# The end of a gated attention + MLP mixer kernel: last exponentials read from the PSUM banks, sums of the last unit by a selector product, and a general path written as a loop

## The chip, the cores and the metric

One Trainium2 chip, one NeuronCore of it. The metric is the device time of one execution in microseconds (us). A kernel is executed several times and the median is taken; one further execution is profiled, and its trace gives start and duration of each instruction.

The engines are PE (TensorE: matrix products into PSUM; a separate row, PEld, shows its weight loads), DVE (VectorE), ACT (ScalarE), POOL (GpSimd) and SP (SyncE, which here issues most DMAs). SBUF and PSUM have 128 partitions; PSUM is used as 8 banks of 128x512 fp32, called bank_1 to bank_8 below.

## The reference

```python
g = _sigmoid((x * gate_w).sum(-1, keepdims=True))
a = _A_ref(x, A_wq, A_wk, A_wv, A_wo)     # attention, 16 heads of 28, one shared k and v
b = _B_ref(x, B_w1, B_w2, B_w3, B_w4)     # layernorm, gelu, shifts by 1 and 2 tokens, MLP
return g * a + (1 - g) * b
...
# in _A_ref:
q = (x @ wq).reshape(B, S, H, Dh).transpose(0, 2, 1, 3)
scores = jnp.einsum("bhqd,bkd->bhqk", q, k) * (Dh ** -0.5)
p = _softmax(scores, axis=-1)
o = jnp.einsum("bhqk,bkd->bhqd", p, v)
```

x is 1 x 2048 x 448 fp32; the result has the same shape.

## The kernel before

The first 400 us or so compute the queries, the keys and values, and all of the branch b, which ends in the tile `x1`. The rest is attention. It runs over 16 **units**; unit u is one block of 512 queries (b = u // 4) for one group of four heads (g = u % 4). The four heads j = 0..3 lie on partitions 32j to 32j+31. A unit has 16 key tiles (kt) of 128 keys, taken two at a time: 8 **stretches** v per unit, 128 stretches in all, written out by the loop over k at L906.

In one stretch, for each kt, `scores` (L851) makes four banks of 128 keys x 512 queries, one for each head, with three products each (a split into high and low parts). `exps` then takes the exponentials: heads 0, 1 and 2 are read from the bank by ACT (L875, 128x512 each); head 3 (`DRAIN`) is copied by DVE from the bank into a tile `pd` (L872), and `late_exps` has ACT do the exponentials of both key tiles of head 3 in one instruction of 128x1024 (L880). `values` (L891) multiplies the exponentials by `vext`, the values with a first column of ones, so row 32j of the result holds the sum of the exponentials of head j. It makes 2 halves of 256 queries; each half is two key tiles times four heads, in fp32, into one bank, and DVE adds the bank to the tile `o` of the unit (L896). `values` of one stretch stands behind the scores of the next.

An fp32 product shows as two records of the PE in the trace (two passes). The four heads write different 32-column groups of the array, and their records overlap.

The finished `o` of unit u is normalised while unit u+1 runs (`sums_begin`, `recip`, `norm`) and multiplied by `wo` in half tiles of 128 tokens x 224 columns by `wo_half` (L813; DVE adds the result into `ot`, L821). Between the values of a stretch and the scores stand one or two of these half jobs; unit 14's eight half jobs stand in stretches 4 to 7 of unit 15.

**The end (L935 to L1016)**, for unit 15, which has no successor to hide behind:

- `values` of stretch 7, two banks (`pvs`), added to `o` in four pieces of 128 queries (L983);
- four PE transposes of `o` against `ident` (L988), so that tokens lie on partitions; reciprocals of the sums from the bank (L951), the product with them into `on4` (L955), four transposes back (L960), four ACT copies into `on` (L961);
- four `wo_job`s of 128 tokens x 448 columns (L813), with the final add on DVE for t = 0, 2, 3 (L971) and on ACT and POOL for t = 1 (L968, L969), and one output DMA each (L973): three issued by SP, one by ACT;
- `check` compares every sum with a limit (L783), `worst` is the least of the results (L1002), a PE transpose puts the 128 of them in a row (L1009), DVE makes the integer `redo` (L1012, L1013), and every engine loads it into a register (L1016) and branches on it (L1019);
- products of a bf16 tile of zeros into an unused bank stand between these steps (`keep_warm`, L980: 12 products).

If `redo` is not 0, all 16 units are computed again with exact row maxima (the **general path**). With these inputs it is not taken: every engine branches over it. It is written out for the 16 units, and stands in the program between the branch and the last few instructions. Counted in the built program, it holds 290 instructions for SP, 2,035 for ACT, 1,570 for DVE, 7,489 for PE and 104 for POOL. Behind it, in `if_false` and `end`, SP waits for its eight DMA semaphores, and the engines meet in a barrier (L1091 in the trace).

Order on each engine is that of the program text; the framework adds the semaphores. `tc.mark_branch_hint_location` at L985 puts one instruction on PE's queue (BRANCH_PREFETCH_HINT) that names the target of the later branch. The code between `with tc.block()` and its end stands in a block of its own, which every engine enters and leaves by an unconditional branch.

## Time and profile before

| | us |
|---|---|
| median of 3 runs | 925.17 |
| the three runs | 923.02, 925.17, 926.17 |
| the profiled execution, its own time | 922.61 |
| its span, first to last instruction | 920.8 |
| PE busy in the span | 909.2 |
| ACT busy | 634.7 |
| DVE busy | 542.2 |
| last exponentials of unit 15 end (L880) | at 905.32 |
| last computing instruction ends (DVE L971) | at 914.72 |

Times of single instructions are given as the start in us from the first instruction, so 905.32 is 15.5 us before the end of the span. The table shows that the median of the runs lies 2.56 us above the profiled execution, and that 1.81 us of the profiled time lie outside its span. Between the end of the last exponentials and the last computing instruction are 9.4 us; from there to the end of the span are 6.08 us, in which no engine computes.

### The profile page before, as it was taken

The numbers are of one execution on the slowest core, as the hardware profiler recorded it, in microseconds if no ns is written. First come the engines' busy times: TensorE is split into PE (matmuls) and PEld (weight loads), VectorE is DVE, ScalarE is ACT, GpSimd is POOL, SyncE is SP. The second block draws the span as 40 slices with busy tenths as digits, with TensorE's granted clock in tenths as the row PEclk, the third lists the DMA queues.
The fourth block names the chain that finished last, engine by engine and source line by source line (L and its number), as shares of the span: only waits on it lengthen the run. The fifth ranks groups of instructions, "written<-read, shape, count | busy, mean of one in ns | idle before, by whom it ended". The sixth has DMA issues, their size and how long they took to land. (4 is left out here: it accounts for less than half of the span.)

```text
span 920.8 us, 23987 instructions
## 1 busy us (share of the span) xinstructions
PE 909.2 (99%) x10039; PEld 643.9 (70%) x10039; DVE 542.2 (59%) x1081; ACT 634.7 (69%) x1134; POOL 105.9 (12%) x135
## 2 busy tenths in 40 slices
PE   9999999999999999999999999999999999999996
PEld 6788888888888888875555566555556555565653
DVE  4664264631435746446666676666666766766664
ACT  5542255322222131259999999999999999999993
POOL 2243200221000530031000000000000000000000
PEclk9999999999999999999999999999999999999999
DMA  9822543220221132110100101100011100110001
GB/s 307 296 65 47 160 147 114 40 66 21 41 70 50 37 97 62 26 60 18 26 25 3 25 15 56 24 26 26 11 37 46 26 6 22 36 45 3 14 14 44
DMA packets 41812, 51.85 MB, mean 56 GB/s; under 512 B 9312, under 2 KB 27552, under 8 KB 41696
## 3 DMA queue, kind: packets, MB, share of 16 engines
q1 hardware_dynamic: 38672, 44.77, 17.0%
q10 hardware_dynamic: 3024, 5.47, 1.7%
q8 instruction: 80, 1.31, 0.6%
q14 instruction: 36, 0.29, 0.1%
HBM read 37.04 MB, written 11.93 MB: 53 GB/s over the span
## 5 line engine op out<-in xcount | busy, mean ns | idle before, releaser
L875 ACT ACTIVATE p<-bank 128x512 f32<-128x512 f32 x768 | 391.0, 623 | 5.8 <-PE bank L851 5.8
L891 PE MATMUL bank<-p,vext 128*32 128x256 f32 x3072 | 243.9, 379 | 2.1 <-ACT p L875 2.1
L891 PE MATMUL bank<-pd,vext 128*32 128x256 f32 x1024 | 242.2, 379 | 0.3 <-ACT pd L880 0.3
L872 DVE COPY pd<-bank 128x512 f32<-128x512 f32 x256 | 176.7, 691 | 54.2 <-PE bank L851 52.5
L891 PEld LDWEIGHTS bank<-p,vext 128*32 128x32 f32 x3072 | 125.1, 110 | 85.8 <-ACT p L875 5.2
L664 ACT ACTIVATE gh<-g 128x512 fp32r<-128x512 f32 x55 | 32.9, 599 | 187.3 <-PE g L135 187.3
L896 DVE TENSOR_TENSOR o<-o,bank 128x256 f32<-128x256 f32 x222 | 93.5, 421 | 90.5 <-ACT p L875 51.0
L880 ACT ACTIVATE pd<-pd 128x1024 f32<-128x1024 f32 x128 | 142.5, 1113 | 0.0
L851 PE MATMUL bank<-qh,kH 30*128 30x512 f32 x1024 | 119.2, 444 | 0.0
L891 PEld LDWEIGHTS bank<-pd,vext 128*32 128x32 f32 x1024 | 111.6, 110 | 1.3 <-ACT pd L880 0.7
L666 DVE TENSOR_TENSOR gl<-gf,gh 128x512 fp32r<-128x512 f32 x55 | 37.9, 689 | 124.5 <-ACT gf L665 124.4
L851 PE MATMUL bank<-qh,kL 28*128 28x512 f32 x1024 | 105.1, 394 | 0.0
L851 PE MATMUL bank<-ql,kH 28*128 28x512 f32 x1024 | 104.4, 389 | 0.0
L851 PEld LDWEIGHTS bank<-qh,kH 30*128 30x128 f32 x1024 | 60.7, 182 | 58.4 <-ACT p L875 47.0
L675 PE MATMUL acc<-w4l,gh 128*128 128x448 f32 x220 | 80.4, 366 | 0.0
L674 PE MATMUL acc<-w4h,gh 128*128 128x448 f32 x220 | 80.3, 365 | 0.0
L676 PE MATMUL acc<-w4h,gl 128*128 128x448 f32 x220 | 80.1, 364 | 0.0
L813 PE MATMUL bank<-wof,on 128*32 128x224 f32 (+1 forms) x992 | 73.1, 370 | 0.3 <-ACT p L875 0.3
L132 PE MATMUL g<-al,w3h 128*128 128x512 f32 x168 | 65.8, 391 | 0.0
L131 PE MATMUL g<-ah,w3h 128*128 128x512 f32 x168 | 65.6, 391 | 0.0
L133 PE MATMUL g<-ah,w3l 128*128 128x512 f32 x168 | 65.5, 390 | 0.0
L851 PEld LDWEIGHTS bank<-ql,kH 28*128 28x128 f32 x1024 | 51.5, 185 | 9.2
(196 smaller groups left out, 1159.0 us busy)
## 6 DMA issues: line engine op xcount, KB each, us to landing
qd<-qf ACTq DMA_DIRECT2D x16, 256.0 KB
qm<-qd SPq DMA_DIRECT2D x16, 256.0 KB
qr<-qd SPq DMA_DIRECT2D x16, 256.0 KB
rb<-rd SPq DMA_DIRECT2D x15, 256.0 KB
x<-in_x_dram SPq DMA_DIRECT2D x4, 896.0 KB
xd<-xt SPq DMA_DIRECT2D x16, 224.0 KB
w34raw<-in_w_dram SPq DMA_DIRECT2D x7, 512.0 KB
out_dram<-ot SPq DMA_DIRECT2D x15, 224.0 KB
```

Source lines behind the costliest of these rows:

```text
L131: nc.tensor.matmul(ps, wh[:, c, :], ah[:, c, :], start=(c == 0), stop=False)
L132: nc.tensor.matmul(ps, wh[:, c, :], al[:, c, :], start=False, stop=False)
L674: nc.tensor.matmul(ps, gh[:, tok], w4h[i][:, k, :], start=(f == 0), stop=False)
L675: nc.tensor.matmul(ps, gh[:, tok], w4l[i][:, k, :], start=False, stop=False)
L676: nc.tensor.matmul(ps, gl[:, tok], w4h[i][:, k, :], start=False, stop=(f == stop))
L813: nc.tensor.matmul(ps[32 * j:32 * j + 32, cols], on_of[u][:, tok], wof[:, g, cols], start=True, stop=True, tile_position=(0, 32 * j))
L851: nc.tensor.matmul(bs[j], w, a, start=(i == 0), stop=(i == 2), tile_position=(32 * j, 0))
L872: nc.vector.tensor_copy(ps[j], bs[j])
L875: behind[kt % 2] = nc.scalar.activation(ps[j], bs[j], AF.Exp, scale=SCALE)
L880: ins = nc.scalar.activation(pd, pd, AF.Exp, scale=SCALE)
L891: nc.tensor.matmul(pv[32 * j:32 * j + 32, q], vext[:, kt, :], p_of[u, kt][j][:, q], start=(kt % 2 == 0), stop=(kt % 2 == 1), tile_position ...
L896: nc.vector.tensor_add(o_of[u][:, q], o_of[u][:, q], pv[:, q])
```

## The change

Everything up to the second last stretch is unchanged: the instructions of all five engines are the same up to there, but for five small POOL memsets that fill two constants at the start of the attention part. The loop stops one stretch earlier (L962 of the new file), and the last stretch and the end are written out anew.

- **Last stretch.** All four heads are read by ACT from the banks: four exponentials of 128x512 for key tile 14, then, for key tile 15, four of the first 256 queries and four of the last 256. The two DVE copies (L872) and the one exponential of 128x1024 (L880) are gone. The values of key tile 14 and of the halves of key tile 15 are separate steps. The half jobs 3 and 7 of unit 14 move behind them.
- **Sums and normalising.** `sel` is a 128x4 tile with ones at (32j, j). The product of a 128-token piece of `o` with `sel` gives the four sums with tokens on partitions. Two pieces make 8 columns, DVE takes their reciprocals and spreads them by a copy to 128x256 (`rx`), two PE products against `ident` bring them back into the layout of `o`, and DVE multiplies `o` by them straight into `on`. The transposes of `o`, the transposes back, the four ACT copies and the 12 `keep_warm` products are gone.
- **The flag.** The product of `worst` with a column of ones counts the tokens that pass; one DVE compare makes `redo`.
- **General path.** One unit (`redo_unit`) in a hardware loop `tc.For_i`, which keeps its running result in a DRAM tile. It holds 77 instructions for SP, 150 for ACT, 121 for DVE, 491 for PE and 29 for POOL between the branch and its target. It is still not taken with these inputs.

ACT, the last stretch. In the rows, p_ and pd_ are tiles of exponentials, bank_ the PSUM banks, and the words in brackets the engines whose semaphores are waited for. Before:

```order
L875 ACTIVATE p_3523<-bank_3504 128x512 [waits PE_49]
L875 ACTIVATE p_3524<-bank_3502 128x512 [waits PE_49]
L875 ACTIVATE p_3525<-bank_3505 128x512 [waits PE_49]
L875 ACTIVATE p_3526<-bank_3508 128x512 [waits DVE_49,PE_49]
L875 ACTIVATE p_3527<-bank_3506 128x512 [waits DVE_49,PE_49]
L875 ACTIVATE p_3528<-bank_3501 128x512 [waits DVE_49,PE_49]
L880 ACTIVATE pd_3536<-pd_3536 128x1024 [waits DVE_49,Activation_49]
```

With the change:

```order
L914 ACTIVATE p_3531<-bank_3504 128x512 [waits PE_49]
L914 ACTIVATE p_3532<-bank_3507 128x512 [waits PE_49]
L914 ACTIVATE p_3533<-bank_3502 128x512
L914 ACTIVATE p_3534<-bank_3505 128x512
L914 ACTIVATE p_3535<-bank_3508 128x256 [waits DVE_49,PE_49]
L914 ACTIVATE p_3536<-bank_3503 128x256 [waits DVE_49,PE_49]
L914 ACTIVATE p_3537<-bank_3506 128x256
L914 ACTIVATE p_3538<-bank_3501 128x256
L914 ACTIVATE p_3535<-bank_3508 128x256
L914 ACTIVATE p_3536<-bank_3503 128x256
L914 ACTIVATE p_3537<-bank_3506 128x256
L914 ACTIVATE p_3538<-bank_3501 128x256
```

Seven instructions became twelve over the same 4,096 columns; head 3's exponentials moved from the end of the queue to the second place of each group of four.

DVE, from the last add of unit 15 to the products with the reciprocals (o_ is the unit's unnormalised result, on_ the normalised one, rr_ the reciprocals, ot_ the output tiles). Before:

```order
L983 TENSOR_TENSOR o_10577<-o_10577,bank_3508 128x128 [waits DVE_49,PE_49,Activation_49]
L983 TENSOR_TENSOR o_10577<-o_10577,bank_3508 128x128
L983 TENSOR_TENSOR o_10577<-o_10577,bank_3503 128x128 [waits DVE_49,PE_49]
L983 TENSOR_TENSOR o_10577<-o_10577,bank_3503 128x128
L984 UNCONDITIONAL_BRANCH x2
L951 RECIPROCAL rr_10978<-bank_3506 128x8 [waits PE_49,Activation_49]
L955 TENSOR_TENSOR on_10979<-bank_3506,rr_10978 128x128 [waits DVE_49]
L955 TENSOR_TENSOR on_10979<-bank_3506,rr_10978 128x128
L951 RECIPROCAL rr_10978<-bank_3501 128x8 [waits PE_49,Activation_49]
L955 TENSOR_TENSOR on_10979<-bank_3501,rr_10978 128x128 [waits DVE_49]
L955 TENSOR_TENSOR on_10979<-bank_3501,rr_10978 128x128
```

With the change, where rx_ is the spread copy of the reciprocals:

```order
L940 TENSOR_TENSOR o_10585<-o_10585,bank_3502 128x256 [waits DVE_49,PE_49,Activation_49]
L827 SCALAR_TENSOR_TENSOR ot_9951<-bank_3504,gg,ot_9951 128x224 [waits PE_49]
L1005 RECIPROCAL rr_10909<-bank_3507 128x8 [waits PE_49]
L1006 COPY rx_10910<-rr_10909 128x256 [waits DVE_49]
L940 TENSOR_TENSOR o_10585<-o_10585,bank_3505 128x256 [waits PE_49,Activation_49]
L1016 TENSOR_TENSOR on_10908<-o_10585,bank_3502 128x128 [waits PE_49]
L1016 TENSOR_TENSOR on_10908<-o_10585,bank_3502 128x128
L1005 RECIPROCAL rr_10909<-bank_3504 128x8 [waits PE_49]
L1006 COPY rx_10910<-rr_10909 128x256 [waits DVE_49]
L1050 UNCONDITIONAL_BRANCH
L827 SCALAR_TENSOR_TENSOR ot_10187<-bank_3505,gg,ot_10187 128x224 [waits PE_49]
L1050 UNCONDITIONAL_BRANCH
```

The first half's reciprocals now stand ahead of the second half's add, two half jobs of unit 14 stand among them, and each reciprocal is followed by a copy.

PE, the same place with the change (the two products of exponentials with vext are the last values of unit 15):

```order
L819 MATMUL bank_3504<-wof,on_10723 32x224 [waits DVE_49]
L819 MATMUL bank_3504<-wof,on_10723 32x224 x3
L1003 MATMUL bank_3507<-sel,o_10585 128x4 [waits DVE_49]
L1003 MATMUL bank_3507<-sel,o_10585 128x4
L936 MATMUL bank_3505<-p_3535,vext 32x256 [waits Activation_49]
L936 MATMUL bank_3505<-p_3537,vext 32x256 [waits Activation_49]
L936 MATMUL bank_3505<-p_3538,vext 32x256 [waits Activation_49]
L936 MATMUL bank_3505<-p_3536,vext 32x256
L1012 MATMUL bank_3502<-ident,rx_10910 128x128 [waits DVE_49]
L1012 MATMUL bank_3502<-ident,rx_10910 128x128
L1003 MATMUL bank_3504<-sel,o_10585 128x4 [waits DVE_49]
L1003 MATMUL bank_3504<-sel,o_10585 128x4
```

The last values of the second half stand behind the selector products of the first, which wait for DVE.

The diff, cut:

```diff
+        sel = s3.tile([P, 4], F32, name="sel")
+        nc.gpsimd.memset(sel, 0.0)
+        for j in range(4):
+            nc.gpsimd.memset(sel[32 * j:32 * j + 1, j:j + 1], 1.0)
+        ones1 = s3.tile([P, 1], F32, name="ones1")
+        nc.gpsimd.memset(ones1, 1.0)
...
+        def redo_unit(i, acc, gd):
...
+        def last_exps(kt, bs, parts):
+            ps = p_of[NU - 1, kt] = {j: turn_of(p_free) for j in READ}
+            for q in parts:
+                for j in READ:
+                    nc.scalar.activation(ps[j][:, q], bs[j][:, q], AF.Exp, scale=SCALE)
...
+        def value(u, kt, q, pv):
+            for j in range(4):
+                nc.tensor.matmul(pv[32 * j:32 * j + 32, q], vext[:, kt, :], p_of[u, kt][j][:, q],
+                                 start=(kt % 2 == 0), stop=(kt % 2 == 1), tile_position=(0, 32 * j))
+
+        def add_value(u, q, pv):
+            nc.vector.tensor_add(o_of[u][:, q], o_of[u][:, q], pv[:, q])
+            banks.append(pv)
...
-        for k in range(NU * NV):
+        for k in range(NU * NV - 1):
...
         def tail_sums(i):
-            nc.vector.reciprocal(rr[:, i], sums_of(i))
-        def tail_on(t):
...
-        def tail_back(t):
...
+            ps = take()
+            for k in range(2):
+                nc.tensor.matmul(ps[:, 4 * k:4 * k + 4], o[:, toks[2 * i + k]], sel, start=True, stop=True)
+            sums = ps[:, 0:8].rearrange("p (k j) -> p k j", k=2)
+            nc.vector.reciprocal(rr[:, i], sums)
+            nc.vector.tensor_copy(rx[:, i], rr[:, i].unsqueeze(3).broadcast_to([P, 2, 4, 32]))
+            return sums, ps
+
+        def tail_spread(i):
+            ps = take()
+            for k in range(2):
+                nc.tensor.matmul(ps[:, toks[2 * i + k]], rx[:, i, k].rearrange("p j d -> p (j d)"), ident,
+                                 start=True, stop=True)
+            for k in range(2):
+                q = toks[2 * i + k]
+                nc.vector.tensor_mul(on_of[u][:, q], o[:, q], ps[:, q])
+            banks.append(ps)
...
+        bs = [scores(u, kt) for kt in (NT - 2, NT - 1)]
+        last_exps(NT - 2, bs[0], [slice(0, 512)])
+        banks.extend(bs[0][j] for j in READ)
+        last_exps(NT - 1, bs[1], HALVES)
+        values(u, v - 1)
+        pvs = [take(), take()]
+        for i, q in enumerate(HALVES):
+            value(u, NT - 2, q, pvs[i])
+        value(u, NT - 1, HALVES[0], pvs[0])
+        add_value(u, HALVES[0], pvs[0])
+        wo_half(u - 1, 3)
+        held = [tail_sums(0)]
+        value(u, NT - 1, HALVES[1], pvs[1])
+        add_value(u, HALVES[1], pvs[1])
+        banks.extend(bs[1][j] for j in READ)
+        tail_spread(0)
+        held.append(tail_sums(1))
         with tc.block():
             tc.mark_branch_hint_location("redo", "LikelyTaken", [mybir.EngineType.PE])
-            keep_warm(5)
...
+            wo_half(u - 1, 7)
+        tail_spread(1)
+        for i in range(2):
+            tail_check(i, *held[i])
         nc.vector.tensor_reduce(worst, good, axis=AX.XY, op=ALU.min)
...
+        wo_job(u, 0, end)
+        tw = bank("worst_t")[0:1, 0:1]
+        nc.tensor.matmul(tw, worst, ones1, start=True, stop=True)
+        nc.vector.tensor_scalar(redo, tw, P - 0.5, None, op0=ALU.is_lt)
+        for t in range(1, 4):
+            wo_job(u, t, end)
         again = nc.values_load(redo, min_val=0, max_val=1)
 
         with tc.If(again > 0, label="redo"):
-            for b in range(NB):
-                for g in range(NG):
...
+            acc = dram.tile([NB, 4, P, D], F32, name="acc")
+            gd = dram.tile([NB, P, 4], F32, name="gd")
+            nc.sync.dma_start(acc.rearrange("b t p d -> p (b t) d"), x1)
+            nc.sync.dma_start(gd.rearrange("b p t -> p b t"), gg.rearrange("p (b t) -> p b t", t=4))
+            with tc.For_i(0, NU, 1) as i:
+                redo_unit(i, acc, gd)
+            nc.sync.dma_start(out[0], acc.rearrange("b t p d -> (b t p) d"))
```

137 lines of the change are left out of this document (52 added, 85 removed).

## The prediction, made before the changed kernel ran

> **What bounds the kernel now.** I read the page first, then the timeline of the last 20 us, then the instructions on the line of the final branch, and last the DMA share behind the last computation. The page:
>
> ```profile
> span 920.8 us, 23987 instructions
> PE 909.2 (99%) x10039; PEld 643.9 (70%) x10039; DVE 542.2 (59%) x1081; ACT 634.7 (69%) x1134; POOL 105.9 (12%) x135
> ```
>
> PE is the bound over the whole. The change leaves 127 of 128 stretches alone, so only the end can answer. There the engines take turns, as the timeline shows (start us, duration, engine, line, count, idle before and its releaser):
>
> ```profile
> 901.33 3.05 ACT L875 ACTIVATE p<-bank 128x512 f32<-128x512 f32 x6 [0.29 <-PE bank L851]
> 902.00 0.96 PE L813 MATMUL bank<-wof,on 128*32 128x224 f32 x16
> 903.43 0.39 PE L891 MATMUL bank<-p,vext 128*32 128x256 f32 x3
> 903.64 0.39 PE L891 MATMUL bank<-p,vext 128*32 128x256 f32 x3
> 904.22 1.10 ACT L880 ACTIVATE pd<-pd 128x1024 f32<-128x1024 f32 x1
> 905.37 0.40 PE L891 MATMUL bank<-pd,vext 128*32 128x256 f32 x1 [0.25 <-ACT pd L880]
> 907.66 0.47 PEld L988 LDWEIGHTS bank<-ident,o 128*128 128x128 f32 x4
> 907.77 0.60 PE L988 MATMUL bank<-ident,o 128*128 128x128 f32 x4
> 908.25 0.21 DVE L951 RECIPROCAL rr<-bank 128x8 f32<-128x8 f32 x1 [0.46 <-PE bank L988]
> 908.50 0.49 DVE L955 TENSOR_TENSOR on<-bank,rr 128x128 f32<-128x128 f32 x2
> 908.84 0.33 PEld L960 LDWEIGHTS bank<-ident,on 128*128 128x128 f32 x2 [0.43 <-DVE on L955]
> 909.54 0.23 DVE L783 SCALAR_TENSOR_TENSOR good<-bank,good 128x8 f32<-128x8 f32 x2
> 909.80 0.19 DVE L1002 TENSOR_REDUCE worst<-good 128x1 f32<-128x32 f32 x1
> 909.96 0.96 PE L813 MATMUL bank<-wof,on 128*32 128x448 f32 x8
> 910.98 0.68 DVE L971 SCALAR_TENSOR_TENSOR ot<-bank,gg,ot 128x448 f32<-128x448 f32 x1 [1.00 <-PE bank L813]
> 912.19 1.71 PE L813 MATMUL bank<-wof,on 128*32 128x448 f32 x16
> 913.30 1.43 DVE L971 SCALAR_TENSOR_TENSOR ot<-bank,gg,ot 128x448 f32<-128x448 f32 x2 [0.48 <-PE bank L813]
> ```
>
> The last values wait for head 3's exponentials, which end at 904.22 + 1.10 = 905.32; the adds, transposes, reciprocals and four output jobs follow in a chain, and the last DVE instruction ends at 913.30 + 1.43 = 914.73. The span ends 6.08 us later. The instructions of the final branch show what fills that (duration min/median/max in ns, first and last start in us):
>
> ```profile
> L1019 SPq EVENT_SEMAPHORE  x8: 17/17/17, 918.9 to 919.4; - x8
> L1019 POOLq COMPARE_BRANCH  x1: 45/45/45, 913.4 to 913.4; - x1
> L1019 PEldq COMPARE_BRANCH  x1: 430/430/430, 913.5 to 913.5; - x1
> L1019 PEldq EVENT_SEMAPHORE  x1: 51/51/51, 914.0 to 914.0; - x1
> L1019 POOLq EVENT_SEMAPHORE  x1: 17/17/17, 914.0 to 914.0; - x1
> L1019 DVEq COMPARE_BRANCH  x1: 72/72/72, 914.7 to 914.7; - x1
> L1019 ACTq COMPARE_BRANCH  x1: 54/54/54, 915.1 to 915.1; - x1
> L1019 SPq COMPARE_BRANCH  x1: 45/45/45, 916.3 to 916.3; - x1
> L1019 DVEq EVENT_SEMAPHORE  x1: 21/21/21, 918.2 to 918.2; - x1
> L1019 ACTq EVENT_SEMAPHORE  x1: 17/17/17, 918.6 to 918.6; - x1
> ```
>
> From the branch to the first instruction behind it DVE needs 3.5 us, ACT 3.5, SP 2.6; POOL, which jumps over 104 instructions, 0.6, and PE, which was told the target, 0.5. DVE, ACT and SP jump over 1,570, 2,035 and 290. DVE and ACT wait there only for their own semaphore, long reached, so their 3.5 us is the price of the long jump. SP is last: 1.9 us of fixed work follows its 918.9.
>
> **The change part by part.** I build the new end from the same instant, 901.33.
>
> *Exponentials.* ACT gives a 128x512 every (904.22 - 901.33) / 6 = 0.48 us. Four for key tile 14 start up to 902.77, the next at 903.25. A 128x256 does not stand in the trace: half the 0.48 is 0.24; half of one whole 128x512 (0.62, below) is 0.31. I take 0.26: a 1024 costs 1.10 and a 512 0.62, so 256 columns more cost about 0.24, and the start-up is mostly hidden in the pitch. The first halves are then done at 903.25 + 4 x 0.26 + 0.1 = 904.4, the second at 905.45 (905.3 to 905.8). ACT's end is not earlier; what changes is that only two steps of values stand behind it.
>
> ```profile
> L875 ACT ACTIVATE p<-bank 128x512 f32<-128x512 f32 x768 | 391.0, 623 | 5.8 <-PE bank L851 5.8
> L896 DVE TENSOR_TENSOR o<-o,bank 128x256 f32<-128x256 f32 x222 | 93.5, 421 | 90.5 <-ACT p L875 51.0 <-PE bank L891 39.5
> L894 DVE COPY o<-bank 128x256 f32<-128x256 f32 x32 | 13.6, 424 | 14.2 <-ACT p L875 7.5 <-PE bank L891 6.7
> L821 DVE SCALAR_TENSOR_TENSOR ot<-bank,gg,ot 128x224 f32<-128x224 f32 x88 | 38.6, 442 | 0.0
> ```
>
> *PE up to the first half.* A step of values (four heads, one pass) takes 0.21 (903.43 to 903.64). From 902.00, where a half job gets its bank now, run 8 steps of stretch 6, 4 of key tile 14 and 2 of the first half: 14 x 0.215 = 3.0, last step issued at 904.8, done at 905.2. The exponentials of 904.4 are in time. DVE adds 0.42: 905.7. The two half jobs that stood at 902.00 (0.96 for both) fill PE's later waits; the two removed copies on DVE are off the path, since DVE waits for PE there.
>
> *Two rounds of sums and spread.* The selector product waits for that add: four loads of 0.117 (0.47 for 4, L988) and the drain, 0.6, so 905.8 to 906.4. Behind it on PE stand the second half's values (two steps, done 906.9), which cost nothing by ACT but wait here for DVE. DVE: reciprocal 0.21, copy 128x256 to rx. No such SBUF copy stands in the trace; the same size from a bank is 0.42, a floor is half of it, 0.21. I take 0.3: 907.0. Second add: 907.45. The spread is two fp32 products of 128 columns, four records like those of L988: 0.6, so 907.1 to 907.7; DVE's two products 0.49 (L955): 908.3. Second selector product 907.7 to 908.3, reciprocal and copy to 908.85; the half job of L1050 and its DVE part (0.44) to 909.3; second spread 908.95 to 909.6.
>
> *Output jobs.* PE takes 0.75 for each (0.96 with its drain). Job 0 follows the second spread: 909.55 to 910.3. DVE does the second pair of products (0.49, to 910.2), checks 0.23, worst 0.19: 910.65, then its add for job 0. PE's product with `worst` waits for that, and jobs 1 to 3 are queued behind it: start 910.85, last done at 910.85 + 3 x 0.75 + 0.2 = 913.3. The last DVE add, 0.68 with its start, ends at 914.1 to 914.2. Against 914.73 that is **0.55 earlier**. Bounds: 1.2 earlier if the copy and the short exponentials take the low ends and the handovers are as short as the 0.09 of L955 to L960; 0.6 later if copy (+0.12 twice) and exponentials (+0.2) take the high ends and the block's branches cost the 0.41 that PE lost there before:
>
> ```profile
> 907.21 0.44 PEld L980 LDWEIGHTS <-warm 128*128 128x128 bf16 x5 [0.41 <-issue]
> ```
>
> *The final branch.* DVE jumps over 121 instructions instead of 1,570, ACT 150, SP 77. POOL's jump over 104 took 0.6, so I price all three at 0.6. SP issues the last output, loads the flag and branches 1.6 us after DVE's end (914.73 to 916.3); with 0.6 it is at its DMA waits 2.2 us after, not 4.2. Then it may have to wait for the outputs to land:
>
> ```profile
> 915.00:916.50 1.50, 0.00 (x0) 0.00 (x0) 0.00 (x0) 0.00 (x0) 0.00 (x0) 1.00 0.99 358
> 916.50:917.00 0.50, 0.00 (x0) 0.00 (x0) 0.00 (x0) 0.00 (x0) 0.00 (x0) 1.00 0.54 189
> 917.50:918.00 0.50, 0.00 (x0) 0.00 (x0) 0.00 (x0) 0.00 (x0) 0.00 (x0) 1.00 0.05 18
> 918.00:918.50 0.50, 0.00 (x0) 0.00 (x0) 0.00 (x0) 0.00 (x0) 0.00 (x0) 1.00 0.00 0
> ```
>
> (The last two numbers are DMA share and GB/s; the 1.00 ahead of them is PE's granted clock.) The engines are full until about 916.7 and silent from 918.0, so the outputs land between 2.1 and 3.3 us after DVE's end. I take 2.6, which is nearer to the end of the full stretch than to the silence, since single late packets make up what follows 917.0: **1.6 earlier** than the 4.2 of now, bounds 0 and 2.0.
>
> The Trainium skill speaks here (Runtime: NRT & Kernel Launch, "Instruction fetch mechanics"): a taken branch whose target lies outside the current window of two pages forces a fetch of the target page, and a page is 16 KiB or 256 instructions. The rows agree with the rule for DVE and ACT. They differ on the page for these engines: queue q14 below moved 0.29 MB in 36 packets, 8 KB each, while q8 has 16 KB.
>
> ```profile
> q8 instruction: 80, 1.31, 0.6%
> q14 instruction: 36, 0.29, 0.1%
> ```
>
> *What is free.* The POOL memsets run at the start of attention, where POOL is 12% busy; `keep_warm` filled pauses of PE, and its loss costs nothing if the clock holds: after PE's last product at 913.9 the rows above still show 1.00 at 918.5, over 4 us later, and no pause of PE in my sum reaches 1 us.
>
> **Sum.** 0.55 + 1.6 = 2.15 us. The profiled execution would go from 922.61 to 920.5, its span from 920.8 to 918.65. The median of the runs is 2.56 above the profiled one, so 925.17 - 2.15 = **923.0**.
>
> **The rivals.**
>
> - *The branch gives nothing.* SP's 2.6 us would be the wait for the landing, or the fetch comes anyway. For it: SP's 290 instructions are far fewer than DVE's, and the row alone does not separate a jump from a DMA wait. Against it: DMA is silent from 918.0 and SP moves at 918.9. Only the 0.55 remains: 924.6. By the skill's 256 instructions a page, SP's target would lie in the next page already now, which speaks for this rival; by the 8 KB packets it would not.
> - *Both parts at their upper ends.* The chain in the end has less waiting than I count, and the outputs land soon after 2.2 us: 1.1 + 2.0 = 3.1, giving 922.1. For it: output 2 of 3 leaves earlier when the jobs run back to back.
> - *PE's clock falls* without the filler products. From the point where a pause is taken as idle, PE's work in the chain doubles: values 0.6, selector 0.6 and 0.6, spreads 1.2, half job 0.4, jobs 3.0, so up to 5 to 6 us more against 2.15 less: 928.5. Against it stands the 1.00 over 4 us of silence.
> - *It does nothing that shows:* the round trips between PE and DVE eat the end's 0.55 and the landing eats the branch: 925.2.
>
> **How the numbers follow.** Forecast 0.50, branch gives nothing 0.17, both upper ends 0.22, clock 0.06, nothing 0.05. What a measurement can tell from no change is about 0.3%, 2.8 us, so faster means under 922.4, slower over 927.9. Faster: all of the upper ends (0.22) and about three tenths of the forecast's cases, where a median of three strays by a us (0.15): 0.37. Slower: the clock and a trace of the rest: 0.07. Same: 0.56. The range: the bounds give 925.17 less 3.2 and plus 0.6, 922.0 to 925.8; the strength of the forecast's middle cuts the top to 925.4, and runs that spread over 3 us (923.02 to 926.17) widen the bottom to 921.0.
>
> **What would show it.** The instruction that follows the final branch starts within 0.7 us on DVE and ACT, and SP's eight waits begin 2.2 to 3 us behind the last DVE add. Twelve exponentials end near 905.5; the last add ends near 914.1; the granted clock stays 1.00; all before 901 is as it was. It is wrong if DVE and ACT still need over 2 us behind the branch, if SP's first wait alone lasts until 4 us after the add, or if the reciprocal-copy-spread rounds end later than 909.6.

## The result, and the profile after

| | before | after |
|---|---|---|
| median | 923.08 us (20 runs, 922.45 to 926.17) | 922.81 us (20 runs, 921.27 to 925.21) |
| ratio, 95% interval | | 0.9991 [0.9984, 0.9999] |
| the profiled execution | 922.61 us, span 920.8 | 921.29 us, span 919.5 |

By the ratio the change gains 0.83 us (0.0009 x 923.08), with 0.1 to 1.5 as its interval; the two medians differ by only 0.27. This is within the 0.3% below which the prediction counts a result as no change, the likeliest of its three cases (0.56). The median of before, 925.17 in the first three runs, is 923.08 over twenty.

The end of the changed kernel, DVE's part of its timeline (start, duration, engine, line, operation, tiles, idle time before it):

```profile
906.00 0.42 DVE L940 TENSOR_TENSOR o<-o,bank 128x256 f32<-128x256 f32 x1 [0.87 <-ACT p L914]
...
907.13 0.21 DVE L1005 RECIPROCAL rr<-bank 128x8 f32<-128x8 f32 x1 [0.34 <-PE bank L1003]
907.37 0.29 DVE L1006 COPY rx<-rr 128x256 f32<-128x256 f32 x1
907.80 0.42 DVE L940 TENSOR_TENSOR o<-o,bank 128x256 f32<-128x256 f32 x1
908.47 0.49 DVE L1016 TENSOR_TENSOR on<-o,bank 128x128 f32<-128x128 f32 x2 [0.25 <-PE bank L1012]
...
910.33 0.48 DVE L1016 TENSOR_TENSOR on<-o,bank 128x128 f32<-128x128 f32 x2 [0.42 <-PE bank L1012]
910.73 0.23 DVE L789 SCALAR_TENSOR_TENSOR good<-bank,good 128x8 f32<-128x8 f32 x2
911.00 0.19 DVE L1056 TENSOR_REDUCE worst<-good 128x1 f32<-128x32 f32 x1
...
913.05 1.44 DVE L1028 SCALAR_TENSOR_TENSOR ot<-bank,gg,ot 128x448 f32<-128x448 f32 x2 [1.05 <-PE bank L819]
```

ACT's part of the same timeline:

```profile
902.00 4.28 ACT L914 ACTIVATE p<-bank 128x512 f32<-128x512 f32 x12 [0.30 <-PE bank L896]
```

and PE's first selector products and second spread:

```profile
906.48 0.61 PE L1003 MATMUL bank<-sel,o 128*128 128x4 f32 x4 [0.22 <-DVE o L940]
...
909.51 0.71 PE L1012 MATMUL bank<-ident,rx 128*128 128x128 f32 x4
```

From the first exponential of the last stretch (902.00) to the end of the last DVE add (913.05 + 1.44 = 914.49) go 12.48 us by the unrounded times; before, 901.33 to 914.73, 13.39. This way is called the **body** below, and what follows the last add, up to the span's end, the **end**: 920.8 - 914.73 = 6.1 us before, 919.5 - 914.49 = 5.0 after. Body 0.91 earlier, end 1.05 earlier: 1.96, of which the span shows 1.3. The rest went ahead of the last stretch (below).

The instructions around the final branch, grouped by line (count, duration in ns, first and last start), in the changed kernel:

```profile
L1066 SPq EVENT_SEMAPHORE  x8: 17/17/17, 917.2 to 918.1; - x8
...
L1066 DVEq COMPARE_BRANCH  x1: 72/72/72, 914.4 to 914.4; - x1
L1066 DVEq EVENT_SEMAPHORE  x1: 21/21/21, 915.0 to 915.0; - x1
L1066 ACTq COMPARE_BRANCH  x1: 54/54/54, 915.3 to 915.3; - x1
L1066 SPq COMPARE_BRANCH  x1: 45/45/45, 916.7 to 916.7; - x1
L1066 ACTq EVENT_SEMAPHORE  x1: 17/17/17, 918.2 to 918.2; - x1
```

and SP's output DMAs, the durations being those of the issue (least, median, most):

```profile
L1030 SPq DMA_DIRECT2D out_dram<-ot x3: 338/344/1173, 912.0 to 914.5; - x3
```

DVE needs 0.6 us for its jump and SP 0.5, where they needed 3.5 and 2.6. ACT still needs 2.9. SP's last issue, 333 ns before, takes 1173. The last of SP's eight waits, the one for the last output, ends at 918.1, and 1.4 us of fixed work follow it, so this wait now sets the end. Windows of the DMA engines (the last three numbers are PE's clock, the DMA share and GB/s):

```profile
914.50:916.50 2.00, 0.00 (x0) 0.00 (x0) 0.00 (x0) 0.00 (x0) 0.00 (x0) 1.00 0.79 283
916.50:917.00 0.50, 0.00 (x0) 0.00 (x0) 0.00 (x0) 0.00 (x0) 0.00 (x0) 1.00 0.61 222
917.00:917.50 0.50, 0.00 (x0) 0.00 (x0) 0.00 (x0) 0.00 (x0) 0.00 (x0) 1.00 0.13 47
917.50:918.00 0.50, 0.00 (x0) 0.00 (x0) 0.00 (x0) 0.00 (x0) 0.00 (x0) 1.00 0.09 24
```

The engines carry much data until 917.0 and then a thin tail, single late parts of the last output. By the packet records the last of these ends at 917.67, and what is left after it is a packet of code; the semaphore for the last part comes at 918.12, 3.63 us behind the last add. This arrival of its last semaphore is meant below where an output **lands**.

**Ahead of the last stretch.** Two starts of the same instruction, the exponential of 128x1024 that stands once in each stretch, 110 stretches apart; before:

```profile
463.29 1.11 ACT L880 ACTIVATE pd<-pd 128x1024 f32<-128x1024 f32 x1
...
891.40 1.10 ACT L880 ACTIVATE pd<-pd 128x1024 f32<-128x1024 f32 x1
```

and after:

```profile
462.87 1.11 ACT L931 ACTIVATE pd<-pd 128x1024 f32<-128x1024 f32 x1
...
892.05 1.10 ACT L931 ACTIVATE pd<-pd 128x1024 f32<-128x1024 f32 x1
```

428.11 us before, 429.18 after. The changed kernel reached this part 0.42 earlier, lost 1.07 in it, and entered its last stretch 0.67 later. The 0.42 says nothing of the change: in two profiles of the kernel before, the first such exponential starts at 407.2 and at 408.8. Together: -0.42 + 1.07 + 0.02 - 0.91 - 1.05 = -1.3, the difference of the spans.

### The profile page after: what moved, and what is told of

Read it like the earlier page. It is cut to its first block, busy times and chain, and to the rows that moved or that the text cites. A ratio compares the mean times of both kernels' runs of the same rounds, so it can differ in the third digit from the quotient of the medians.

```text
span 919.5 us, 23981 instructions
## 1 busy us (share of the span) xinstructions
PE 909.0 (99%) x10036; PEld 643.5 (70%) x10036; DVE 541.9 (59%) x1078; ACT 635.0 (69%) x1135; POOL 104.5 (11%) x141
## 4 chain that ended last, share of the span: by engine, by line
PE 95%; ACT 3%; DVE 1%; DMA 0%; issue 0%; ACTq 0%; DVEq 0%
PE bank L936 23%; PE bank L896 21%; PE bank L819 7%; PE acc L675 5%; PE acc L674 5%; PE acc L676 5%; PE g L132 4%; PE g L131 4%; PE g L133 4%; ACT p L926 2%; PE hs L454 1%; PE hs L455 1%; PE g L135 1%; PE g L134 1%; PE h L131 1%; PE h L133 1%
```

## The experiments

All times of a run's body and end are from its own profile; each run's ratio is against runs of the kernel before on the same chip. The labels are the names in the table at the end of this section.

**body_only: the new end without the loop.** The general path is written out again, all else is as in the changed kernel.

```diff
         with tc.If(again > 0, label="redo"):
-            with tc.For_i(0, NU, 1) as i:
-                redo_unit(i, acc, gd)
+            for b in range(NB):
+                for g in range(NG):
+                    ...
```

> The changed end with the general path written out as before. Main theory: two separate gains. From the first exponential of the last stretch to the end of the last DVE add 12.5 us as with the change (13.4 before), and from there to the end of the span 6.1 us as before, with 2.5 to 3.5 us behind the final branch on SP, DVE and ACT; time about 0.9 us under before (ratio 0.999). Rival 1: the shorter program also shortens the end itself, then 13.4 returns. Rival 2, for the attention part: moving the tiles by 64 bytes makes each stretch slower, then the mean stretch is 3.90 us as with the change; if the drift is only from run to run, it can be anything from 3.88 to 3.91.

Measured: 923.96 us, ratio 1.000 [0.999, 1.0009]. Body 12.48, as with the change. SP's issues and the branch:

```profile
L1030 SPq DMA_DIRECT2D out_dram<-ot x3: 343/343/1301, 913.0 to 915.5; - x3
```

```profile
L1066 SPq EVENT_SEMAPHORE  x8: 17/17/17, 920.3 to 920.9; - x8
...
L1066 SPq COMPARE_BRANCH  x1: 45/45/45, 917.8 to 917.8; - x1
L1066 DVEq EVENT_SEMAPHORE  x1: 21/21/21, 919.0 to 919.0; - x1
```

The end is 6.77 us, not 6.1: SP's last issue takes 1.30 us instead of 0.33, SP reaches its branch later by that, and then pays the long jump, 2.5 us. So 0.5 to 0.7 of the new body's 0.9 is given back in the end (6.77 against 6.3 and 6.1 in the two profiles of the kernel before), to a slow issue that nothing in the diff names.

**loop_only: the old end with the loop.** The reverse edit: the end of the kernel before, the general path as `redo_unit` in a loop.

> The old end with the general path as a loop. Main theory: 13.4 us from the first exponential of the last stretch to the last DVE add as before, then 5.0 us or less to the end (6.1 before), with 0.5 to 0.7 us behind the branch on SP and DVE; ACT jumps over 137 instructions here and 150 with the change, so its 2.9 us may go or stay; ratio 0.999. Rival (the wait of SP is the landing of the output): 6.1 stays, ratio 1.000. Attention: the tiles stand at the old places, so 3.89 us per stretch if places matter.

Measured: 922.70 us, ratio 0.9984 [0.9973, 0.9994]. The body is 13.40 (903.37 to 916.76), the end 5.54, not the 5.0 or less of the main theory.

```profile
L1058 SPq EVENT_SEMAPHORE  x8: 17/17/17, 918.8 to 920.9; - x8
...
L1058 DVEq EVENT_SEMAPHORE  x1: 21/21/21, 917.3 to 917.3; - x1
L1058 SPq COMPARE_BRANCH  x1: 45/45/45, 918.3 to 918.3; - x1
L1058 ACTq EVENT_SEMAPHORE  x1: 17/17/17, 920.7 to 920.7; - x1
```

SP's jump takes 0.5 and its last issue 333 ns, so its eight waits begin 2.1 us behind the last add. They end at 4.2: SP now stands and waits for the last output. The loop does shorten the jumps of DVE and SP (ACT's, over 137 instructions, takes 3.6), and behind them lies the landing, not at 2.6 us but at 4.1 here.

The times of these two runs say something that the profiles of the end do not: the loop alone (0.9984) gains at least as much as the new end and the loop together (0.9991, and 0.9983 in a second measurement, below), and the new end alone gains nothing (1.000). The intervals overlap, so this is no more than a sign that the 0.9 us of the new body are lost again elsewhere in the kernel.

**hint_act: ACT is told the branch's target too.**

```diff
-            tc.mark_branch_hint_location("redo", "LikelyTaken", [mybir.EngineType.PE])
+            tc.mark_branch_hint_location("redo", "LikelyTaken", [mybir.EngineType.PE, mybir.EngineType.Activation])
```

> The changed kernel with the branch hint on ACT's queue too. Theory: ACT's 2.9 us behind the final branch are a fetch of instructions, and fall to 0.5 to 0.6. If ACT holds the end, the 5.0 us from the last DVE add to the end become 4.4 to 4.7, and the time is 0.3 to 0.6 us under the changed kernel; if SP's own chain (output, flag, eight DMA waits) holds it, 5.0 stays though ACT is early. Rival: ACT's 2.9 us wait for its output's transfer, then the hint changes nothing.

Measured: 922.13 us, ratio 0.9986 [0.9977, 0.9994]; body 12.48, end 5.06. ACT's jump still takes 2.7 us (915.6 to 918.3), and SP's last issue 1228 ns. A hint like PE's did nothing here for ACT; what it does for PE no run shows.

**old_places: the new small tiles behind the large ones in SBUF.** The allocations of `sel` and `ones1`, with their memsets, stand behind those of the `pd` tiles, so that the large tiles keep the addresses of the kernel before.

> The changed kernel with the two new constants allocated behind the tiles of exponentials, so that those stand at the addresses of before. If the move by 64 bytes made the stretches 3.90 instead of 3.89 us, they are 3.89 again and the time is about 1 us under the changed kernel (ratio 0.998 to before). If the drift was only from run to run, the time is that of the changed kernel (ratio 0.999).

Measured: 923.07 us, ratio 0.9987 [0.9974, 1.0001]; body 12.48, end 5.20. 49 stretches of attention (about 701 to 891 us in the kernel before) take 190.96 us, 190.53 in the kernel before, 191.06 in the changed one: the addresses of the tiles of exponentials are not what slows them.

**act_first: output job 0, not 1, over ACT and POOL.**

```diff
-            if t == 1:
+            if t == 0:
                 nc.scalar.activation(y, ps, AF.Copy, scale=gg[:, n:n + 1])
...
-            queue = nc.scalar if t == 1 else nc.sync
+            queue = nc.scalar if t == 0 else nc.sync
```

> Of the four output jobs the first, not the second, goes over ACT and POOL, so ACT issues its output about 1 us earlier and SP issues the other three. In the changed kernel ACT's issue starts 0.29 us before the last DVE add's end and SP's third issue, 0.32 us behind it, took 1.17 us instead of 0.34; in the kernel before, with 0.72 us between them, it took 0.33. Theory A (the third issue is slow because it comes right behind ACT's): SP's third issue takes 0.34 us, SP's eight waits begin 0.5 us or more earlier than 2.7 us behind the last DVE add, the last output lands up to 0.5 us earlier than 3.6 us behind that add, and the end (last DVE add to the span's end) goes from 5.03 to 4.5 to 4.9 us. Theory B (it is slow for another reason, such as a code fetch of SP): still about 1.2 us, end 5.0. Theory C (the issue is quick again but the landing is set by late packets): issue 0.34, end still 5.0. The way from the first exponential of the last stretch to the last DVE add stays 12.5 us in all.

Measured: 922.56 us, ratio 0.9987 [0.9979, 0.9996]; body 12.48, end 5.0.

```profile
L1030 SPq DMA_DIRECT2D out_dram<-ot x3: 338/434/1202, 914.4 to 916.3; - x3
```

One issue is still slow, now SP's second (1202 ns); the third takes 434. ACT's issue lay 0.7 us ahead of the slow one, as far as in the kernel before. Theory A falls; the numbers are those of theory B, whatever the reason.

**worst_late: the product with `worst` and the flag behind job 2.**

```diff
-        tw = bank("worst_t")[0:1, 0:1]
-        nc.tensor.matmul(tw, worst, ones1, start=True, stop=True)
-        nc.vector.tensor_scalar(redo, tw, P - 0.5, None, op0=ALU.is_lt)
-        for t in range(1, 4):
-            wo_job(u, t, end)
+        wo_job(u, 1, end)
+        wo_job(u, 2, end)
+        tw = bank("worst_t")[0:1, 0:1]
+        nc.tensor.matmul(tw, worst, ones1, start=True, stop=True)
+        nc.vector.tensor_scalar(redo, tw, P - 0.5, None, op0=ALU.is_lt)
+        wo_job(u, 3, end)
```

> The product with worst and the flag that DVE makes of it go behind the third output job instead of the first. Theory A: PE stood still from the end of job 0's issue (910.15 + 0.75 = 910.9) to 911.25 for DVE's worst; the jobs run back to back and the way from the first exponential of the last stretch to the last DVE add goes from 12.49 to 12.15 us. Theory B: job 0's products were only drained by 911.1 and the wait cost 0.15 at most: 12.35 to 12.5. The end stays 5.0 (third issue of SP about 1.2 us).

Measured: 922.55 us, ratio 0.9989 [0.9979, 1.0]. PE's three first jobs now run in one piece (its timeline):

```profile
910.71 2.46 PE L819 MATMUL bank<-wof,on 128*32 128x448 f32 x24
```

and the body is 12.17 us, 0.32 shorter, as theory A said. But the end is 5.9, not 5.0. All three issues of SP are quick (332 to 343 ns), and yet:

```profile
L1067 SPq EVENT_SEMAPHORE  x8: 17/17/17, 916.8 to 919.3; - x8
```

The last output lands at 919.3, 4.5 us behind the last add (914.73). What the DMA engines carried from 917.2 to 918.2 (queue and kind, packets, MB, share of 16 engines):

```profile
DMA packets 7, 0.03 MB, mean 32 GB/s; under 512 B 1, under 2 KB 5, under 8 KB 5
...
q8 instruction: 1, 0.02, 6.0%
q1 hardware_dynamic: 5, 0.01, 4.9%
q14 instruction: 1, 0.01, 2.6%
```

Five packets of output stand beside two of code. By the packet records, the q8 packet (PE's, 16 KB; PE's load of the flag came 1.8 us later here against the last add, and with it PE's branch) ran from 917.22 to 918.18 for 0.96 us, where a row of the output takes 0.074; the last row of the output started at 918.17, as that packet ended. This fits a last output that waited behind a packet of code; that both stood on the same DMA engine is not shown, since the records do not name the engine.

**pad_act: ACT's branch 42 instructions further on in its code.** Nothing of the computation depends on the added copies.

```diff
             nc.vector.tensor_sub(gl, gf, f32(gh))
+            if b == NB - 1:
+                for i in range(3):
+                    nc.scalar.copy(pad[:, 1 + f:2 + f], pad[:, 0:1])
             return gh, gl
```

> 42 tiny ACT copies are added in the last block of the third weight stage (three behind each gf), where ACT waits 3.85 us for PE each time, so that ACT's final branch lies 42 instructions further on in its code. The general path that it jumps over stays the same 150. Theory A (a jump is quick where the target lies in the present or the next piece of 128 instructions, the 8 KB of a q14 packet; ACT's 150 cross two borders from where it stood, DVE's 121 and SP's 77 only one): ACT moves on 0.6 us behind the branch instead of 2.9. The end stays at 5.0, because the landing of the last output bounds it, or gains up to 0.4 us where the fetch no longer shares the DMA engines with the outputs. Theory B (150 is too far wherever it starts, or ACT waits for something else): 2.9 us again. The copies themselves cost under 0.1 us on the path.

Measured: 922.68 us, ratio 0.999 [0.9981, 1.0]; body 12.48, end 4.96.

```profile
L1072 SPq EVENT_SEMAPHORE  x8: 17/17/17, 918.8 to 919.6; - x8
...
L1072 ACTq COMPARE_BRANCH  x1: 54/54/54, 916.8 to 916.8; - x1
L1072 ACTq EVENT_SEMAPHORE  x1: 17/17/17, 917.3 to 917.3; - x1
```

ACT jumps over the same 150 instructions in 0.5 us instead of 2.9. So not the distance alone decides, but where in its code the branch stands, as theory A has it. By the packet records no packet of code comes between ACT's branch and its next instruction here; in the changed kernel two of q14 do, though the records do not say for which engine. The end hardly moves, since ACT is not what SP waits for last.

The Trainium skill (Runtime: NRT & Kernel Launch, "Instruction fetch mechanics") says that a taken branch stalls if its target is outside the present window of two pages. This run agrees with that rule. The page size that it gives, 16 KiB or 256 instructions, would make a jump of 150 quick from any place, if the window is the present page and the next. With half of that, the 8 KB of a q14 packet, the changed kernel and this run both fit, if the borders lie so that the 150 instructions crossed two of them and cross one now. Where the borders lie no run shows, so the 8 KB are a guess that fits.

**early_load: the flag is loaded into the registers right behind its product**, ahead of jobs 1 to 3; only the branch stays at the end.

```diff
         nc.vector.tensor_scalar(redo, tw, P - 0.5, None, op0=ALU.is_lt)
+        again = nc.values_load(redo, min_val=0, max_val=1)
         for t in range(1, 4):
             wo_job(u, t, end)
-        again = nc.values_load(redo, min_val=0, max_val=1)
```

> The engines load the flag of the final branch into their registers right behind its product, ahead of output jobs 1 to 3, instead of behind them; only the branch itself stays at the end. In seven profiles SP's issue was slow (0.9 to 1.3 us) just where another engine's load of the flag began 0.05 us behind the start of that issue while outputs were under way (ACT's load at the third issue, DVE's at the second where the first job goes over ACT), and quick (0.33) where the load had begun before it. Theory A (the load that begins during the issue holds it up): SP's third issue 0.34 us, SP at its branch 0.5 us behind the last DVE add instead of 2.2, its eight waits from 1.0; the landing of the last output, 3.4 to 3.6 us behind the add so far, then shows alone: 2.5 to 3.5, the end 4.0 to 5.0 us instead of 5.03. Theory B (the issue waits for room in the queue or for something else): third issue still 0.9 to 1.3 us, SP's waits from 2.0 on. ACT's exponent-free job 1 starts 0.3 us later by its load, which is off the path. From the first exponential of the last stretch to the last DVE add 12.5 us.

Measured: 923.74 us, ratio 0.9992 [0.9981, 1.0003]. SP's issues are all quick (333 to 342 ns) and its waits begin 0.9 us behind the add; the last output lands at 3.3, the end is 4.7. But the body is 13.78. PE's timeline shows where that went:

```profile
912.70 0.19 PE L1059 MATMUL bank<-ones,worst 128*1 128x1 f32 x2
914.04 2.46 PE L819 MATMUL bank<-wof,on 128*32 128x448 f32 x24 [1.15 <-DVE redo L1060]
```

PE has to load the flag as well, and its jobs 1 to 3 stand behind that load: 1.15 us of waiting, which the expectation did not see.

**best_a: early_load, act_first and pad_act together.**

> The early load of the flag, the first output job over ACT and POOL instead of the second, and the 42 copies that put ACT's final branch further on, together. ACT then branches about 1 us before the last DVE add and its jump needs no code from outside its window, so the only instruction packets left beside the last output are those of PE and of the program's end. Theory A (late packets of the last output are those that queue behind instruction fetches on the same DMA engine): all 16 parts of the last output land by 2.5 to 2.9 us behind the last DVE add instead of 3.4 to 3.6, end 4.0 to 4.4 us, time about 0.8 us under the changed kernel's. Theory B (late packets come anyhow): landing 3.4 to 3.6, end 4.9 to 5.1. Body 12.5 us in both.

Measured: 923.95 us, ratio 1.0001 [0.9989, 1.0013]. Body 13.47 (the same wait of PE, 0.84 us), end 4.15.

```profile
L1072 SPq EVENT_SEMAPHORE  x8: 17/17/17, 918.7 to 920.6; - x8
```

The last add ends at 917.83, so the last output lands 2.75 us behind it. Here PE's code packet had ended 0.8 us ahead of the last add, ACT's jump was quick (0.5 us), and the windows show no tail:

```profile
917.85:919.85 2.00, 0.00 (x0) 0.00 (x0) 0.00 (x0) 0.00 (x0) 0.00 (x0) 1.00 0.72 260
919.85:920.35 0.50, 0.00 (x0) 0.00 (x0) 0.00 (x0) 0.00 (x0) 0.00 (x0) 1.00 0.05 18
920.35:920.85 0.50, 0.00 (x0) 0.00 (x0) 0.00 (x0) 0.00 (x0) 0.00 (x0) 1.00 0.00 0
```

The end is the one that theory A forecast; the body eats the gain. But the records give another reason than theory A's. The last output lands in 16 parts, each with its own semaphore record. In the changed kernel the middle one of them lands 2.69 us behind the last add and the last one 0.94 later; here it is 1.86, and the last one 0.89 later. So the late parts trail as they did before, and the whole output lands 0.83 earlier, just as much as SP's last issue ends earlier (0.36 us behind the add instead of 1.20). The quick issue alone is not enough, though: in early_load it ends at 0.36 too, and the middle part lands at 2.36. There ACT's output was issued 0.3 us ahead of the last add, here 2.4 us.

**best_b: the same, with `worst`, flag and load behind job 1.**

> As the kernel before in this list, with the product with worst, the flag and its load put behind the second output job instead of the first, so that PE does not stand still for DVE (0.32 us, as the run with that product behind the third job showed: 12.17 us instead of 12.49). PE's own branch, and with it its 16 KB instruction packet, come about 0.5 us later against the last DVE add than in the changed kernel (where the packet ran from 0.53 before the add to 0.45 behind it), and still ahead of the last output's packets. Theory A: body 12.17 us, end as that of the kernel before in this list (4.0 to 4.4). Theory B (SP's load of the flag now sits between its first and second issue and delays the outputs, or PE's packet meets the last output as it did when the product stood behind the third job): body 12.17, end 4.8 us or more.

Measured: 924.64 us, ratio 1.0005 [0.9993, 1.0016]. Landing 2.8, end 4.2 as in best_a, though SP's last issue took 689 ns; body 13.78, since PE waits 1.46 us for the flag, now ahead of jobs 2 and 3. The stall moved with the load. SP's issue, though slower than in best_a, ended 0.72 us behind the add, and the middle part landed at 2.23: again 1.5 us behind the end of the issue, as in the changed kernel and in best_a.

**after_again and before_again: both kernels once more, unaltered.**

> The changed kernel once more, unaltered, to see how far its own profile repeats. In its first profile the attention's stretches came every 3.899 us against 3.890 in the kernel before, 1.1 us over the whole. Theory A (this is a difference between executions): another pitch, anywhere between 3.887 and 3.90, and a time ratio of 0.9975 to 0.9985. Theory B (the change costs the attention 1.1 us): 3.899 again. In both: first exponential of the last stretch to last DVE add 12.49 us, end 5.0, SP's third issue 1.2 us.

> The kernel before once more, unaltered. The attention's stretches came every 3.890 us in its first profile and 3.888 in the one kernel with the old end, but every 3.893 to 3.900 in eight profiles of kernels with the new end. Theory A (a difference between executions): anywhere from 3.887 to 3.90. Theory B (the new end costs the attention 0.5 to 1.1 us): 3.888 to 3.891 again. First exponential of the last stretch to last DVE add 13.40 us, end 6.0 to 6.2.

Measured: the changed kernel 922.10 us, ratio 0.9983 [0.9973, 0.9993], body 12.48, end 4.9, SP's last issue 933 ns. The kernel before, in one profiled execution, 924.40 us, body 13.40, end 6.3, SP's last issue 713 ns. The 49 stretches took 190.88 and 190.51 us, 3.896 and 3.888 each: the kernel before repeats its pitch, and every kernel with the new end is slower, as theory B of before_again has it.

All profiles in one table (us; the last output's middle and last part and PE's packet of code against the end of the last DVE add; the parts are by the semaphore records, since SP does not wait for them everywhere):

| kernel | 49 stretches | body | end | SP's last issue | last output: middle part | last part (lands) | PE's packet |
|---|---|---|---|---|---|---|---|
| before | 190.53 | 13.39 | 6.1 | 0.33 | 2.4 | 3.6 | -0.1 to 1.1 |
| before_again | 190.51 | 13.40 | 6.3 | 0.71 | 2.4 | 4.0 | 0.5 to 1.5 |
| loop_only | 190.54 | 13.40 | 5.5 | 0.33 | 2.4 | 4.1 | 0.7 to 1.6 |
| after | 191.06 | 12.48 | 5.0 | 1.17 | 2.7 | 3.6 | -0.5 to 0.5 |
| after_again | 190.88 | 12.48 | 4.9 | 0.93 | 2.5 | 3.4 | -0.6 to 0.3 |
| body_only | 190.81 | 12.48 | 6.8 | 1.30 | 2.8 | 3.9 | -0.4 to 0.7 |
| hint_act | 190.80 | 12.48 | 5.1 | 1.23 | 2.7 | 3.7 | -0.5 to 0.5 |
| old_places | 190.96 | 12.48 | 5.2 | 1.28 | 2.8 | 3.8 | -0.4 to 0.6 |
| act_first | 190.85 | 12.48 | 5.0 | 0.43 (second 1.20) | 2.6 | 3.6 | -0.9 to 0.2 |
| worst_late | 191.09 | 12.17 | 5.9 | 0.33 | 2.4 | 4.5 | 2.5 to 3.5 |
| pad_act | 191.06 | 12.48 | 5.0 | 1.29 | 2.8 | 3.6 | -0.6 to 0.7 |
| early_load | 191.07 | 13.78 | 4.7 | 0.33 | 2.4 | 3.3 | -1.8 to -0.9 |
| best_a | 191.06 | 13.47 | 4.2 | 0.33 | 1.9 | 2.8 | -1.8 to -0.8 |
| best_b | 191.09 | 13.78 | 4.2 | 0.69 | 2.2 | 2.8 | -0.7 to 0.4 |

No kernel here is clearly faster than the changed one. One that has the quick landing of best_a without PE's wait was not tried.

## Why the prediction came out as it did

The forecast was 923.0 us and the median 922.81. That they agree is luck: the base was 2.1 us too high, the gain was forecast too large by more than 1 us, and the two misses offset each other.

**The base.** "The median of the runs is 2.56 above the profiled one" rested on three runs. Over twenty it is 0.47 above (923.08 against 922.61). With this base the forecast gain of 2.15 would have given 920.9, below the stated range. Against the profiled execution the forecast was 920.5 and the measurement 921.29, so 0.8 of the gain is missing there, and 1.3 by the ratio (2.15 - 0.83).

**The body: right in its mechanism, its size too small.** 0.55 was forecast, 0.91 came, and within 0.02 of it in all seven profiles with the change's order of products and jobs. The instruction prices held to about 0.1 us: selector product 0.61 (0.6 taken), copy 0.29 (0.3), spread 0.71 (0.6); the second spread was done 8.22 us behind the first exponential (910.22 - 902.00; forecast 909.6 - 901.33 = 8.27). What was sized wrong is the way from there on: the checks and `worst` were done at 9.19 (forecast 9.32), job 1 could start at 9.25 (forecast 9.52), and the last add ended 0.78 us behind PE's last product. For this step the prediction says 0.68, yet goes from 913.3 to 914.1 or 914.2, 0.1 to 0.2 more than its own figures give. The copy and the short exponentials took their middle values, not the bounds. PE's clock stayed at 1.00 without the filler products, as taken, through the end of all fourteen profiles; but the reason given for it, the 4 us of silence at 1.00, was weaker than it looked (last section).

**The final branch: the mechanism right on DVE and SP, wrong on ACT.** DVE's jump went from 3.5 to 0.6 us, SP's from 2.6 to 0.5. "I price all three at 0.6" failed for ACT, 2.9 us: in pad_act the same 150 instructions took 0.5 from another place, which fits a jump past the code that was already there. By the prediction's own test ("It is wrong if DVE and ACT still need over 2 us behind the branch") this step fell for ACT. It cost little, because SP's wait for ACT comes behind the landing: with ACT quick the end was 4.96.

**The landing is the term of the sum that was mis-sized.** 2.6 us behind the last add was taken, because "single late packets make up what follows 917.0". That is where the middle part landed (2.7). But SP waits for the last part, not for the bulk: 3.6 in the changed kernel, 3.4 to 4.5 in the eight profiles with the new end and the flag loaded at the end, 2.8 in best_a and best_b. The bound of 3.3, the silence of the engines from 918.0, was too low as well: in the kernel before the last packet of output ends 3.1 us behind the add, and its semaphore comes at 3.6. The gain of the branch was therefore 1.05, not 1.6 (1.4 between the second profiles of both kernels). SP's waits began 2.7 us behind the add, not 2.2, because its last issue took 0.84 more (1.17 against 0.33). The late start of the waits was not what set the end: in early_load they began at 0.9, and the landing still held SP until 3.3. The slow issue itself did delay the landing, since the output it issues comes later: by 0.3 us if early_load is the measure, by 0.8 if best_a is.

**What was called free was not.** "All before 901 is as it was" failed. 49 stretches take 190.51 to 190.54 us in the three profiles with the old end and 190.80 to 191.09 in the eleven with the new one; over 110 stretches 428.11 against 429.18 in the first profiles. That is 0.5 to 1.1 us lost, and in the first profiles it takes back about half of the 1.96 us that body and end gained. The order of the instructions in this part is the same in both kernels, with the same kinds of waits. The loss is spread evenly, 0.005 to 0.01 us in each stretch. The general path is not the cause (loop_only 190.54, body_only 190.81), nor are the addresses of the tiles of exponentials (old_places 190.96). What the new end brings besides, six POOL memsets (not five, as is said above), other places of small tiles and of the code, was not taken away one by one. The cause is open.

**The rivals.** "The branch gives nothing" is refuted by body_only against the changed kernel: 6.8 and 5.0 us of end, with the same body. Of "both upper ends" the body came near (0.91 of 1.1), the landing did not. The clock did not fall in the end. "The landing eats the branch" was true for a third: it took 0.55 of the 1.6.

## What to carry to other kernels

Where a kernel's end is a branch over code that is not taken, count the instructions from branch to target on each engine and see which engines are waited for last: shortening the path helped only up to the landing of the last output, and padding ACT's code by 42 instructions was as good for its jump as a shorter path. Take the time of an output's landing from its last semaphore, not from the end of the full DMA windows. And look at what else uses the DMA engines just then: a 16 KB packet of code took as long as 13 rows of output (0.96 us against 0.074).

## What the runs showed of the hardware that was not expected

**A DMA issue that takes three times as long.** In nine profiles one issue of SP took 0.69 to 1.30 us instead of 0.33. In eight of them PE's 16 KB packet of code had begun 0.2 to 0.8 us ahead of it and was still under way, and the issue ended 0.3 to 0.75 us behind that packet; in before_again a packet of 8 KB was under way, and PE's began 0.43 us into the issue. In four of the five profiles without a slow issue no packet was under way as it began, worst_late, early_load and best_a among them, where the moved flag moves PE's packet; in the first profile of the kernel before two were, PE's (0.15 us old) and one of 8 KB (0.25 us old), and the issue was quick. The other guess, that another engine's load of the flag holds the issue up, does not fit before_again and best_b, where no such load began in it.

The attention part of the same fourteen traces (from 440 us on) has more such cases. Of SP's issues of `qr<-qd`, 256 KB each, the 23 that began with PE's packet under way took 1.18 to 1.78 us, the 118 that met no packet of code 0.33 to 0.43. The 30 output issues there that began with an 8 KB packet under way took 0.33 to 0.34, so it is PE's packet that goes with the slow issues. Not every issue is held: 59 issues of `rd<-rr`, 8 KB each, began with PE's packet under way and took 0.31 to 0.34, and so did ACT's output issue in six profiles (0.34 to 0.35). This is a coincidence in time, though a frequent one; no run changed the packet alone, and why only some issues are slow is open.

**Late parts of an output behind code.** In worst_late the last row of the output started as PE's packet ended, and the output landed 1.7 us later than in best_a, where PE's packet had ended before the last add.

**A quick jump depends on the place of the branch.** The same 150 instructions took ACT 2.9 us in the changed kernel and 0.5 in pad_act.

**A clock that falls at a short pause, in some executions.** At the start of the attention part PE pauses for 0.46 us in all fourteen profiles. In three of them, body_only, old_places and act_first, the granted clock fell to half in this pause and stayed there for 3.4 us, and one stretch took 1.2 to 1.3 us longer than in the other eleven. Windows of 3.5 us that hold the pause, body_only first and the changed kernel below it (length, busy time of PE, PEld, DVE, ACT and POOL, PE's clock, DMA share, GB/s):

```profile
408.40:411.90 3.50, 3.04 (x33) 1.39 (x32) 1.12 (x2) 3.50 (x7) 1.33 (x2) 0.51 0.03 9
```

```profile
407.93:411.43 3.50, 3.04 (x53) 1.94 (x56) 1.56 (x4) 3.50 (x7) 1.42 (x2) 1.00 0.03 8
```

So one execution can be about 1.1 us slower than another with the pauses and the code of this part the same, and ratios that differ by 0.001 may hold some of that. Why it happens in some executions only, no run shows. Behind PE's last product the clock fell after 2.1 us (after_again) to 5.3 us (the changed kernel's first profile). The prediction argued from one execution in which it held for over 4 us; that it also held in the pauses of the end, up to 1.46 us of PE in best_b, the runs show, but not that it must.
